# A fused kernel of retention attention, a soft mixture of experts and a bilinear block: PSUM handed out in tiles of two banks in the attention and in single banks behind it

## The chip, the cores and the metric

The kernel runs on one core of a Trainium2 chip, in one launch. The metric is the device time of that launch in microseconds (us); lower is better. The core has five engines that run side by side and wait for each other with semaphores: TensorE (PE in the profile; PEld is its weight load), VectorE (DVE), ScalarE (ACT), GpSimd (POOL) and SyncE (SP), which here only issues transfers. PE writes its products into PSUM, a memory of eight banks of 128 partitions x 512 float32 values; DVE and ACT read them from there.

## The reference

Three blocks, one behind the other, all in float32:

```python
# attention, 8 batches x 8 heads x 576 positions x 64
scores = (q @ k.T) / 8;  out = (scores * decay(i - j)) @ v        # causal, no softmax
x = out as (4608 tokens, 512 features)
# soft mixture of experts: 8 experts x 4 slots = 32 slots
logits = x @ phi
d = softmax over the tokens of logits
slot_in = d.T @ x;  slot_out[e] = relu(slot_in[e] @ w1[e]) @ w2[e]
x = softmax over the slots of logits @ slot_out
# bilinear block
y = (((x @ m1) * (x @ m2)) @ w3) @ w_out
```

## The kernel before

**Attention.** The 36 units are blocks of 128 tokens; 32 are main units, every ninth is a tail of half the work. In iteration u of the loop (`for u in range(NU)`) PE does, in this order: the product of unit u with the values (`emit_pv`, L280), the state update of unit u+1 (`emit_state`, L294), the scores of unit u+2 (`emit_qk`, L251), transposes (`emit_turns`, L213 and L217) and the part of unit u+1 that comes from the state (`emit_inter`, L314). DVE multiplies what PE left: `emit_xt` scales unit u's output (L328, into `xts`), `emit_p` puts the mask and decay on the scores of unit u+2 (L262, into `pm`). Both do it bank by bank, with two products each for a main unit: scores lie in banks 0 and 1, the output in banks 5 and 3 (of which 256 columns each). Order within an engine is the order of the code; nothing is rescheduled.

**Weights beside it.** The weights of the bilinear block come as 40 pieces in 64-bit floats and are converted beside the attention and the experts: ACT L489 and L491, DVE L490, L492, L484 (`conv_list`), POOL L510 (`add`), and for `wo` and `w3` also ACT L515 (`copy`) and POOL L520 (`sub`).

**Softmax over the tokens.** Every four units there are logits (`emit_logits`, L350, then three small DVE operations), exponentials on ACT, and a running sum `zacc` of one column (`emit_z`, L428) and running slots `acc` (`emit_slots`, `add_slots`, L445). Behind the loop the last logits, transposes (L340), slots and sums are finished: `zb` (L865, from `zacc` and `beta`), the product L866, L872 from `acc`, and `slotm`, from which the first expert starts (L587).

**Experts.** Per expert `emit_l1` (L587), `emit_l2` (L606), with weights that are loaded into every place that comes free (`load_expert`, L570), and products `w3 @ w_out` in between (`emit_Ws`, L551). A cast of w3 (ACT L515) waits until the L551 products on the place that it overwrites are done.

**Pairs.** Since the bilinear block acts on combinations of 32 slots, products of pairs of slots are built: L976 (`sot` with m1 into bank 7, then with m2 into bank 6), DVE transposes L982, and for each block `cb` of features DVE L1020, L1021, L1022 (`pairs`, in banks 7 and 2 in turn), ACT L1023, DVE L1027 (`pairs_low`), and 12 products on PE (`g_mm`, L1035). Behind block 0 stand 16 products into bank 6 (L1065). POOL prepares the first token tile meanwhile (`pair_prep`: L632, ACT L633, L635, then L628, ACT L629, L630).

**Last stage.** Nine token tiles T of four outputs each: for each T four products L1101, then per output 12 products L1110 to L1112, an eviction by ACT (L1114) and a store. The outputs go through the eight banks in the order below, so that a T with an even number begins with bank 7 and the T before it ends with bank 6.

**Banks.** Six banks are tiles of their own; banks 6 and 7 are the halves of one tile `pair`, which holds transposes in the attention:

```python
bank = [psum.tile([128, 512], F32, name=f"bank{i}") for i in range(6)]
pair = psum.tile([128, 1024], F32, name="pair")
bank += [pair[:, 0:512], pair[:, 512:1024]]
...
misc[:] = [bank[6], bank[7], bank[2], bank[4]]      # behind the attention: small products, in turn
...
return bank[(7, 2)[cb % 2]].rearrange("p (a b) -> p a b", b=32) if cb else ptmp[0][0]      # sums(cb)
...
obs = [bank[(7, 4, 2, 0, 1, 5, 3, 6)[(4 * T + tb) % 8]] for tb in range(4)]                # last stage
```

Of the kernel before, what the change touches and what calls it, by code (L numbers as in the profile page):

```python
# [9 lines left out]
F32 = mybir.dt.float32  # L10
# [6 lines left out]
ALU = mybir.AluOpType  # L17
# [14 lines left out]
def retention_softmoe_bilinear(  # L32
# [15 lines left out]
    nc = tc.nc  # L48
    const = ctx.enter_context(tc.tile_pool(name="const", bufs=1))
    tmp = ctx.enter_context(tc.tile_pool(name="tmp", bufs=1))  # L50
    psum = ctx.enter_context(tc.tile_pool(name="psum", bufs=1, space=bass.MemoryType.PSUM))
    dram = ctx.enter_context(tc.tile_pool(name="dram", bufs=1, space=bass.MemoryType.DRAM))

    expt = dram.tile([64 * NT, 512], F32, name="expt")
    bank = [psum.tile([128, 512], F32, name=f"bank{i}") for i in range(6)]
    pair = psum.tile([128, 1024], F32, name="pair")
    bank += [pair[:, 0:512], pair[:, 512:1024]]
    pools = {}

    def open_pool(name, side="left"):  # L60
        cm = tc.tile_pool(name=name, bufs=1, side=side, reuse_waits="tile")
        pools[name] = (cm, cm.__enter__())

    def close_pool(name):
        pools.pop(name)[0].__exit__(None, None, None)

    def new(pool, name, n, dt=F32, **kw):
        return pools[pool][1].tile([128, n], dt, name=name, **kw)

    cst = const.tile([128, 128 + 32 + 128], F32, name="cst")  # L70
    ident, isum = cst[:, 0:128], cst[:, 128:160]
# [64 lines left out]
    def tail(u):  # L136
        return items[units[u][0]][1] == 4
# [7 lines left out]
    def block_of(u):  # L145
        return items[units[u][0]][1]
# [76 lines left out]
    def qk_view(u, h):  # L223
        return bank[6 + h if u == 1 else h]
# [10 lines left out]
    def p_main(u):  # L235
        return p_places[u % 2].rearrange("p (h k t) -> p h k t", h=2, k=4)
# [17 lines left out]
    def emit_p(u):  # L254
        if tail(u):
            nc.vector.tensor_tensor(
                out=p_tail(u), in0=qk_view(u, 0).rearrange("p (x k i) -> p x k i", x=2, k=4),
                in1=ptail.unsqueeze(1).to_broadcast([128, 2, 4, 64]), op=ALU.mult,
            )
            return  # L260
        for h in range(2):
            nc.vector.tensor_tensor(  # L262
                out=p_main(u)[:, h], in0=qk_view(u, h).rearrange("p (k t) -> p k t", k=4), in1=mask_sb.unsqueeze(1).to_broadcast([128, 4, 128]), op=ALU.mult,
            )

    def emit_pv(u):
        x = units[u][1]
# [51 lines left out]
        return last  # L319

    def emit_xt(u):
        for r in range(2):
            ps = bank[(5, 3)[r]][:, 0:256].rearrange("p (k t) -> p k t", k=2)
            o, f = xts[u % 6][:, r::2], xtab_sb[block_of(u) % 4][:, r::2]
            if tail(u):
                o, ps = (t.rearrange("p k (x i) -> p k x i", x=2) for t in (o, ps))
                f = f[:, :, 0:64].unsqueeze(2).to_broadcast([128, 2, 2, 64])
            nc.vector.tensor_tensor(out=o, in0=ps, in1=f, op=ALU.mult)  # L328

    L = {"cc": []}  # L330
    misc = [bank[6], bank[7], bank[2]]
# [91 lines left out]
    def emit_z(T):  # L423
        _, al, zt = st[T]
        if T == 0:
            nc.vector.tensor_copy(zacc, zt)
        else:
            nc.vector.scalar_tensor_tensor(out=zacc, in0=zacc, scalar=al, in1=zt, op0=ALU.mult, op1=ALU.add)  # L428

    def emit_slots(T, add=True):  # L430
        dt = st["dt", T]
# [36 lines left out]
    def load_pieces():  # L468
        while nl[0] < len(pieces) and nl[0] < done[0] + NRAW:
            load_piece(nl[0])  # L470
            nl[0] += 1
# [167 lines left out]
    with tc.manual_schedule():  # L639
# [178 lines left out]
        free.extend([*kb, *p_places, s_place, kt_place])  # L818
        load_expert(4)
        load_pieces()  # L820
        misc[:] = [bank[6], bank[7], bank[2], bank[4]]
        nc.gpsimd.memset(slotm, 0.0)
        emit_logits(T)
# [272 lines left out]
        for T in range(NT):  # L1096
# [5 lines left out]
            for tb in range(4):  # L1102
# [12 lines left out]
                for o, i in stores(4 * T + tb):  # L1115
                    nc.sync.dma_start(out=o, in_=os[i])
        close_pool("place")


# [73 lines left out]
```

## Time and profile before

| | us |
|---|---|
| median of 3 runs | 412.31 (411.59 to 412.42) |
| the profiled execution's own time | 410.99 |
| its span in the trace | 409.3 |
| PE busy | 381.5 (93%) |
| DVE busy | 265.5 (65%) |
| ACT busy | 197.9 (48%) |
| POOL busy | 171.9 (42%) |

Shares of busy time are means over stages with different limits: the attention lasts to about 162 us, the experts to about 257, the pairs to about 295, the last stage to the end. The granted clock of PE is full in all 40 slices of the span. The mean share of the DMA engines is high until about 250 us and low behind that.

### The profile page before, as it was taken

To read this page: it belongs to the slowest core of one execution; us is meant where nothing else is said; L and a number is where in the kernel's file an instruction comes from. 1 tells how busy PE (TensorE), PEld (TensorE's weight loads), DVE (VectorE), ACT (ScalarE), POOL (GpSimd) and SP (SyncE) were. 2 spreads that over 40 slices of the span, in tenths; PEclk is the share of its full clock that TensorE was granted. 3 is DMA by queue.
4 is the path that set the end of the run, shared out by engine and by line. 5 is a ranking of instruction groups with operands and counts; after the bars stand their busy time and mean duration, and the time that the engine had idled before them with its cause. 6 is when DMAs were issued, how large, how long until landed. Compare 5 with 4: busy or idle time off the path is not lost.

```text
span 409.3 us, 11039 instructions
## 1 busy us (share of the span) xinstructions
PE 381.5 (93%) x4447; PEld 284.0 (69%) x4447; DVE 265.5 (65%) x504; ACT 197.9 (48%) x416; POOL 171.9 (42%) x158
## 2 busy tenths in 40 slices
PE   6999979999999998899999889989899999999996
PEld 4888867877988887565555444658587777777774
DVE  4659999999898996429757640469766434445500
ACT  2347777676767765235444412224444353544332
POOL 2635675655454463026335331126634333443320
PEclk9999999999999999999999999999999999999999
DMA  7999998799889887999999999680168979899434
GB/s 243 316 355 336 310 325 278 234 393 373 266 270 338 268 302 266 336 410 323 409 410 408 408 408 317 154 161 2 51 130 204 232 178 239 227 208 222 135 78 103
DMA packets 48211, 108.75 MB, mean 266 GB/s; under 512 B 7584, under 2 KB 10016, under 8 KB 48160
## 3 DMA queue, kind: packets, MB, share of 16 engines
q1 hardware_dynamic: 47008, 107.85, 82.1%
q8 instruction: 35, 0.57, 0.6%
q10 hardware_dynamic: 1152, 0.20, 0.3%
q14 instruction: 16, 0.13, 0.1%
HBM read 97.41 MB, written 10.62 MB: 264 GB/s over the span
## 4 chain that ended last, share of the span: by engine, by line
PE 60%; DVE 18%; DMA 15%; SPq 2%; issue 2%; ACT 2%; POOL 1%; ACTq 0%; POOLq 0%; DVEq 0%
PE bank L1110 6%; PE bank L1111 6%; PE bank L1112 6%; PE bank L551 5%; PE bank L251 5%; PE bank L280 5%; DMA kr<-in_v 4%; PE bank L314 3%; DVE pm L262 3%; DMA kt<-in_ew 3%; DMA k<-in_ew 2%; DMA expt<-et 2%; DVE vals L484 2%; PE pair L1110 2%; DMA xts<-in_ew 2%; PE bank L294 2%
## 5 line engine op out<-in xcount | busy, mean ns | idle before, releaser
L630 POOL TENSOR_TENSOR cc<-mw_sb,cc 128x512 fp32r<-128x512 f32 x36 | 46.0, 1296 | 58.6 <-ACT cc L629 58.6
L510 POOL TENSOR_TENSOR vals<-vals,msb 128x512 int32<-128x512 int32 x24 | 30.8, 1285 | 54.6 <-DVE vals L484 43.9
L551 PE MATMUL bank<-wop,w3p 128*128 128x512 f32 x192 | 50.5, 405 | 0.0
L262 DVE TENSOR_TENSOR pm<-bank,msb 128x512 f32<-128x512 f32 x62 | 39.8, 683 | 10.1 <-PE bank L251 9.8
L551 PEld LDWEIGHTS bank<-wop,w3p 128*128 128x128 f32 x192 | 34.4, 189 | 15.0 <-issue 8.7
L629 ACT CAST cc<-mw_sb 128x512 fp32r<-128x512 f32 x36 | 22.2, 616 | 43.5 <-DVE mw_sb L628 34.8
L251 PE MATMUL bank<-q,kt 64*128 64x128 f32 x496 | 36.4, 285 | 0.9 <-issue 0.9
L628 DVE TENSOR_TENSOR mw_sb<-lga,raw 128x512 f32<-128x512 f32 x32 | 29.3, 955 | 12.3 <-POOL cc L630 12.0
L280 PE MATMUL bank<-pm,v 128*64 128x128 f32 x512 | 35.4, 279 | 0.9 <-issue 0.6
L520 POOL TENSOR_TENSOR w3p<-vals,w3p 128x512 fp32r<-128x512 f32 x16 | 20.6, 1287 | 35.0 <-ACT w3p L515 33.1
L510 POOL TENSOR_TENSOR mw_sb<-mw_sb,msb 128x512 int32<-128x512 int32 x16 | 20.4, 1277 | 33.0 <-DVE mw_sb L484 23.4
L251 PEld LDWEIGHTS bank<-q,kt 64*128 64x128 f32 x496 | 30.3, 187 | 3.7 <-issue 1.6
L1110 PE MATMUL bank<-w3p,cc 128*128 128x512 f32 x81 | 32.0, 395 | 0.0
L280 PEld LDWEIGHTS bank<-pm,v 128*64 128x64 f32 x512 | 27.4, 136 | 6.2 <-issue 4.2
L1112 PE MATMUL bank<-w3p,cc 128*128 128x512 f32 x81 | 31.5, 389 | 0.0
L1111 PE MATMUL bank<-w3p,cc 128*128 128x512 f32 x81 | 31.5, 389 | 0.0
L218 ACT COPY kt<-pair 128x512 f32<-128x512 f32 x26 | 15.3, 589 | 27.4 <-PE pair L217 27.4
L491 ACT ACTIVATE msb<-raw 128x512 int32<-128x512 uint32 x40 | 28.0, 699 | 0.0
L190 POOL TENSOR_TENSOR k<-kr,msb 128x512 f32<-128x512 f32 (+1 forms) x30 | 25.6, 876 | 4.4 <-DMA kr<-in_v 2.6
L314 PE MATMUL bank<-q,st 64*64 64x128 f32 (+1 forms) x512 | 22.3, 269 | 4.7 <-DVE xts L328 4.2
L1035 PE MATMUL bank<-w,wop 128*128 128x512 f32 x96 | 23.4, 396 | 2.7 <-DVE wop L1027 2.7
L1114 ACT ACTIVATE mw_sb<-bank,rz 128x512 f32<-128x512 f32 x27 | 18.5, 686 | 12.7 <-PE bank L1112 6.4
(254 smaller groups left out, 818.5 us busy)
## 6 DMA issues: line engine op xcount, KB each, us to landing
q<-in_q SPq DMA_DIRECT2D x20, 512.0 KB, 6.3
raw<-expt SPq DMA_DIRECT2D x36, 256.0 KB, 4.3
kr<-in_v SPq DMA_DIRECT2D x16, 512.0 KB, 6.3
v<-in_v SPq DMA_DIRECT2D x16, 512.0 KB, 6.7
raw<-in_m SPq DMA_DIRECT2D x16, 512.0 KB, 6.3
raw<-in_w SPq DMA_DIRECT2D x16, 512.0 KB, 6.1
out_x<-mw_sb SPq DMA_DIRECT2D x64, 128.0 KB, 2.5
k<-in_ew SPq DMA_DIRECT2D x14, 512.0 KB, 10.1
```

Of the source, the lines that this page charges most:

```text
L251: last = nc.tensor.matmul(out=ps[:, p], lhsT=ktb[u % 2][a, p], rhs=Q[a, :, x, p], start=True, stop=True)
L262: nc.vector.tensor_tensor(out=p_main(u)[:, h], in0=qk_view(u, h).rearrange("p (k t) -> p k t", k=4), in1=mask_sb.unsqueeze(1).to_broadcast ...
L280: last = nc.tensor.matmul(out=xt_view(p)[side(p, h)], lhsT=v_tile(u)[:, 1 - h, x, p], rhs=p_main(u)[:, h, p], start=(block_of(u) == 0 and ...
L314: last = nc.tensor.matmul(out=xt_view(p)[side(p, h), 64 * y:64 * y + 64] if tail(u) else xt_view(p)[side(p, h)].rearrange("p (c i) -> p c ...
L491: lambda: nc.scalar.activation(out=p.bitcast(I32), in_=lo, func=ACTF.Copy, scale=2.0 ** -29),
L510: nc.gpsimd.tensor_tensor(out=ti, in0=ti, in1=parts[j % 2].bitcast(I32), op=ALU.add)
L551: nc.tensor.matmul(out=ps, lhsT=x, rhs=y, start=(k8 == 0 and part == 0), stop=(k8 == 7 and part == 2))
L628: eng.tensor_tensor(out=e, in0=x, in1=y[:, m], op=ALU.mult)
L630: nc.gpsimd.tensor_tensor(out=cl[m], in0=e, in1=ch[m], op=ALU.subtract)
L1110: nc.tensor.matmul(out=ob, lhsT=ch[m][:, sl], rhs=gh[m], start=False, stop=False)
L1111: nc.tensor.matmul(out=ob, lhsT=ch[m][:, sl], rhs=gl[m], start=False, stop=False)
L1112: nc.tensor.matmul(out=ob, lhsT=cl[m][:, sl], rhs=gh[m], start=False, stop=(m == 3))
```

## The change

PSUM becomes a pool that is opened twice. In the attention it holds three tiles of two banks (`scores`, `output`, `pair`) and two of one (`one`, `state`); the list `bank` maps the old numbers onto their halves. `emit_p` and `emit_xt` make one product of each pair of them, over both banks (tails stay as they were). Behind the attention the pool is closed and opened again with eight tiles of one bank. Apart from that `emit_z` moves from DVE to ACT.

```diff
--- before.py
+++ after.py
@@ -48,17 +48,13 @@
     nc = tc.nc
     const = ctx.enter_context(tc.tile_pool(name="const", bufs=1))
     tmp = ctx.enter_context(tc.tile_pool(name="tmp", bufs=1))
-    psum = ctx.enter_context(tc.tile_pool(name="psum", bufs=1, space=bass.MemoryType.PSUM))
     dram = ctx.enter_context(tc.tile_pool(name="dram", bufs=1, space=bass.MemoryType.DRAM))
 
     expt = dram.tile([64 * NT, 512], F32, name="expt")
-    bank = [psum.tile([128, 512], F32, name=f"bank{i}") for i in range(6)]
-    pair = psum.tile([128, 1024], F32, name="pair")
-    bank += [pair[:, 0:512], pair[:, 512:1024]]
     pools = {}
 
-    def open_pool(name, side="left"):
-        cm = tc.tile_pool(name=name, bufs=1, side=side, reuse_waits="tile")
+    def open_pool(name, side="left", **kw):
+        cm = tc.tile_pool(name=name, bufs=1, side=side, reuse_waits="tile", **kw)
         pools[name] = (cm, cm.__enter__())
 
     def close_pool(name):
@@ -66,6 +62,12 @@
 
     def new(pool, name, n, dt=F32, **kw):
         return pools[pool][1].tile([128, n], dt, name=name, **kw)
+
+    open_pool("psum", space=bass.MemoryType.PSUM)
+    scores, output, pair = (new("psum", n, 1024) for n in ("scores", "output", "pair"))
+    one, state = (new("psum", n, 512) for n in ("one", "state"))
+    b2 = lambda t: (t[:, 0:512], t[:, 512:1024])
+    bank = [*b2(scores), one, output[:, 512:1024], state, output[:, 0:512], *b2(pair)]
 
     cst = const.tile([128, 128 + 32 + 128], F32, name="cst")
     ident, isum = cst[:, 0:128], cst[:, 128:160]
@@ -258,10 +260,10 @@
                 in1=ptail.unsqueeze(1).to_broadcast([128, 2, 4, 64]), op=ALU.mult,
             )
             return
-        for h in range(2):
-            nc.vector.tensor_tensor(
-                out=p_main(u)[:, h], in0=qk_view(u, h).rearrange("p (k t) -> p k t", k=4), in1=mask_sb.unsqueeze(1).to_broadcast([128, 4, 128]), op=ALU.mult,
-            )
+        nc.vector.tensor_tensor(
+            out=p_places[u % 2].rearrange("p (g t) -> p g t", g=8), in0=(pair if u == 1 else scores).rearrange("p (g t) -> p g t", g=8),
+            in1=mask_sb.unsqueeze(1).to_broadcast([128, 8, 128]), op=ALU.mult,
+        )
 
     def emit_pv(u):
         x = units[u][1]
@@ -319,13 +321,17 @@
         return last
 
     def emit_xt(u):
+        o, f = xts[u % 6], xtab_sb[block_of(u) % 4]
+        if not tail(u):
+            by = lambda t: t.rearrange("p (k r) t -> p r k t", r=2)
+            nc.vector.tensor_tensor(out=by(o), in0=output.rearrange("p (r k t) -> p r k t", r=2, k=4)[:, :, 0:2], in1=by(f), op=ALU.mult)
+            return
         for r in range(2):
-            ps = bank[(5, 3)[r]][:, 0:256].rearrange("p (k t) -> p k t", k=2)
-            o, f = xts[u % 6][:, r::2], xtab_sb[block_of(u) % 4][:, r::2]
-            if tail(u):
-                o, ps = (t.rearrange("p k (x i) -> p k x i", x=2) for t in (o, ps))
-                f = f[:, :, 0:64].unsqueeze(2).to_broadcast([128, 2, 2, 64])
-            nc.vector.tensor_tensor(out=o, in0=ps, in1=f, op=ALU.mult)
+            ps = bank[(5, 3)[r]][:, 0:256].rearrange("p (k x i) -> p k x i", k=2, x=2)
+            nc.vector.tensor_tensor(
+                out=o[:, r::2].rearrange("p k (x i) -> p k x i", x=2), in0=ps,
+                in1=f[:, r::2, 0:64].unsqueeze(2).to_broadcast([128, 2, 2, 64]), op=ALU.mult,
+            )
 
     L = {"cc": []}
     misc = [bank[6], bank[7], bank[2]]
@@ -425,7 +431,7 @@
         if T == 0:
             nc.vector.tensor_copy(zacc, zt)
         else:
-            nc.vector.scalar_tensor_tensor(out=zacc, in0=zacc, scalar=al, in1=zt, op0=ALU.mult, op1=ALU.add)
+            nc.scalar.activation(out=zacc, in_=zacc, func=ACTF.Identity, scale=al, bias=zt)
 
     def emit_slots(T, add=True):
         dt = st["dt", T]
@@ -818,6 +824,9 @@
         free.extend([*kb, *p_places, s_place, kt_place])
         load_expert(4)
         load_pieces()
+        close_pool("psum")
+        open_pool("psum", space=bass.MemoryType.PSUM)
+        bank[:] = [new("psum", f"bank{i}", 512) for i in range(8)]
         misc[:] = [bank[6], bank[7], bank[2], bank[4]]
         nc.gpsimd.memset(slotm, 0.0)
         emit_logits(T)
@@ -1115,6 +1124,7 @@
                 for o, i in stores(4 * T + tb):
                     nc.sync.dma_start(out=o, in_=os[i])
         close_pool("place")
+        close_pool("psum")
 
 
 # ---- launch: one core; inputs laid out for the transfers, output as the reference has it ----
```

Three places, as the instructions stand in the built programs (a number behind a name tells buffers apart; what stands in brackets is waited for).

PE in the last stage, from one token tile to the next: `gs` and `cs` are the operands of L1101, `cc` those of L1110 (now L1119). Before:

```order
L1112 MATMUL pair_73<-g3_3491,cc13_3490 128x512
L1101 MATMUL pair_73<-gs_3492,cs_3482 128x512 [waits DVE_49,Activation_49]
L1101 MATMUL bank4_71<-gs_3492,cs_3482 128x512 [waits DVE_49]
L1101 MATMUL bank2_69<-gs_3492,cs_3482 128x512
L1101 MATMUL bank0_67<-gs_3492,cs_3482 128x512
L1110 MATMUL pair_73<-w3p_81,cc00_3483 128x512
```

and now:

```order
L1121 MATMUL bank6_2626<-g3_3437,cc13_3436 128x512
L1110 MATMUL bank7_2627<-gs_3438,cs_3428 128x512 [waits DVE_49]
L1110 MATMUL bank4_2624<-gs_3438,cs_3428 128x512 [waits DVE_49]
L1110 MATMUL bank2_2622<-gs_3438,cs_3428 128x512
L1110 MATMUL bank0_2620<-gs_3438,cs_3428 128x512
L1119 MATMUL bank7_2627<-w3p_79,cc00_3429 128x512 [waits Activation_49]
```

The wait for ACT at the first product is gone; the one at `cc` was implied by it before.

DVE in the stage of the pairs, blocks 1 and 2 (`bank4` and `msb` are the factors). Before:

```order
L1022 TENSOR_TENSOR bank2_69<-bank2_69,mw_sb_79 128x480 [waits DVE_49]
L1020 TENSOR_TENSOR mw_sb_79<-msb_86,bank4_71 128x480
L1021 TENSOR_TENSOR pair_73<-bank4_71,msb_86 128x512 [waits PE_49]
L1022 TENSOR_TENSOR pair_73<-pair_73,mw_sb_79 128x480 [waits DVE_49]
L1027 TENSOR_TENSOR wop_80<-bank2_69,wop_80 128x512 [waits Activation_49]
```

and now:

```order
L1031 TENSOR_TENSOR bank2_2622<-bank2_2622,mw_sb_77 128x480 [waits DVE_49]
L1029 TENSOR_TENSOR mw_sb_77<-msb_84,bank4_2624 128x480
L1030 TENSOR_TENSOR bank7_2627<-bank4_2624,msb_84 128x512
L1031 TENSOR_TENSOR bank7_2627<-bank7_2627,mw_sb_77 128x480 [waits DVE_49]
L1036 TENSOR_TENSOR wop_78<-bank2_2622,wop_78 128x512 [waits Activation_49]
```

The product into bank 7 (now L1030) no longer waits for PE.

ACT behind the attention, from `beta` to the first expert's `hr`. Before:

```order
L852 ACTIVATE beta_2757<-mn_2701,negm_2755 128x1 [waits DVE_49]
L515 CAST w3p_81<-vals_84 128x512 [waits PE_49]
L515 CAST w3p_81<-vals_84 128x512 [waits PE_49,Pool_49]
L592 ACTIVATE hr_2820<-bank0_67 128x256 [waits DVE_49,PE_49]
L559 CAST w0_2826<-bank5_72 128x512 [waits Activation_49]
```

and now:

```order
L861 ACTIVATE beta_2703<-mn_2647,negm_2701 128x1 [waits DVE_49]
L521 CAST w3p_79<-vals_82 128x512 [waits PE_49]
L521 CAST w3p_79<-vals_82 128x512 [waits PE_49,Pool_49]
L434 ACTIVATE zacc_76<-zacc_76,zt_2656,al_2659 128x1 [waits Activation_49]
L598 ACTIVATE hr_2766<-bank0_2620 128x256 [waits DVE_49,PE_49]
L565 CAST w0_2772<-bank5_2625 128x512 [waits Activation_49]
```

The sum `zacc` stands behind both casts of w3.

## Rows read from the trace of the kernel before

**Rows 1.** Chain of waits, in time: start us, us, piece.
```profile
70.31 0.67 DVE xts L328 x2
70.98 1.20 DVE pm L262 x2
...
216.24 11.03 DMA kt<-in_ew
```

**Rows 2.** Timeline, PE, last stage: start us, us, instruction [idle before, releaser].
```profile
307.19 0.39 PE L1112 MATMUL bank<-g,cc 128*128 128x512 f32 x1
307.51 0.73 PE L1101 MATMUL bank<-gs,cs 64*128 64x512 f32 x3
...
318.96 0.39 PE L1112 MATMUL pair<-g,cc 128*128 128x512 f32 x1
320.18 0.50 PE L1101 MATMUL pair<-gs,cs 64*128 64x512 f32 x1 [0.83 <-ACT mw_sb L1114]
```

**Rows 3.** Timeline, ACT, last stage.
```profile
319.44 0.69 ACT L1114 ACTIVATE mw_sb<-pair,rz 128x512 f32<-128x512 f32 x1 [1.65 <-issue]
```

**Rows 4.** Waits, 262 to 409 us: us in total, times, longest.
```profile
PE pair L1101 <- ACT mw_sb L1114: 3.3, 4, 0.8
```

**Rows 5.** Timeline, all engines, stage of the pairs.
```profile
260.97 1.93 PE L976 MATMUL pair<-mw_sb,sot 128*32 128x256 f32 x32 [0.64 <-DVE mw_sb L982]
...
269.75 3.84 PE L1065 MATMUL pair<-w,gs 128*64 128x512 f32 x16
...
273.63 0.70 DVE L1021 TENSOR_TENSOR pair<-bank,msb 128x512 f32<-128x512 f32 x1 [2.54 <-PE pair L1065]
...
275.67 15.59 PE L1035 MATMUL bank<-w,wop 128*128 128x512 f32 x66 [0.25 <-DVE wop L1027]
...
278.70 2.65 POOL L635 TENSOR_TENSOR cs<-mw_sb,cs 32x512 fp32r<-32x512 f32 x2 [8.90 <-ACT cs L633]
...
292.73 2.56 PE L1035 MATMUL bank<-w,wop 128*128 128x512 f32 x10 [1.47 <-DVE wop L1027]
```

**Rows 6.** Timeline, DVE, attention.
```profile
43.47 1.17 DVE L490 TENSOR_SCALAR vals<-vals 128x512 f32<-128x512 f32 x1
...
66.90 1.24 DVE L428 SCALAR_TENSOR_TENSOR zacc<-zacc,al,zt 128x1 f32<-128x1 f32 x1
...
77.51 0.42 DVE L490 TENSOR_SCALAR mw_sb<-mw_sb 128x512 f32<-128x512 f32 x1
...
152.65 0.90 DVE L428 SCALAR_TENSOR_TENSOR zacc<-zacc,al,zt 128x1 f32<-128x1 f32 x1
```

**Rows 7.** Timeline, POOL, attention.
```profile
43.06 1.30 POOL L520 TENSOR_TENSOR wop<-vals,wop 128x512 fp32r<-128x512 f32 x1
...
66.84 1.27 POOL L520 TENSOR_TENSOR wop<-vals,wop 128x512 fp32r<-128x512 f32 x1
```

**Rows 8.** Waits, 20 to 160 us.
```profile
PE bank L314 <- DVE xts L328: 3.4, 5, 1.3
```

**Rows 9.** Timeline, all engines, behind the attention.
```profile
164.52 1.06 PE L434 MATMUL pair<-xg,dt 128*32 128x512 f32 x8 [0.57 <-DVE mt L356]
...
166.19 0.30 ACT L377 ACTIVATE al<-mn,nm 128x1 f32<-128x1 f32 x1
...
170.27 0.33 PE L418 MATMUL pair<-cst,dd 128*128 128x128 f32 x1 [0.68 <-ACT xg L341]
...
172.41 0.28 DVE L865 TENSOR_SCALAR zb<-zacc,beta 128x128 f32<-128x128 f32 x1
...
172.86 3.70 PE L551 MATMUL bank<-wop,w3p 128*128 128x512 f32 x15
172.97 0.75 DVE L445 SCALAR_TENSOR_TENSOR acc<-acc,al,bank 128x512 f32<-128x512 f32 x1 [0.28 <-PE bank L434]
...
176.42 0.62 ACT L515 CAST w3p<-vals 128x512 fp32r<-128x512 f32 x1 [2.17 <-PE bank L551]
...
176.54 1.20 PE L872 MATMUL bank<-ib,acc 128*128 128x32 f32 x12
```

## The prediction

> **What bounds the kernel now.** I read the chain of waits first, then the waits by pair of engines, then the timelines of the stages in which the chain changes its engine. The chain runs through DVE in part of the attention (products L328 and L262 beside the conversions), through transfers in the second half of the experts (a load of 11.03 us at 216.24), and through PE in the last stage [rows 1, 2]. So the change has to be priced four times: in the attention, behind it, in the stage of the pairs, and in the last stage.
>
> The reader should look for one thing above all: waits that name the tile `pair` although the two instructions use different halves. In the last stage PE begins an even token tile with bank 7. At 307.51, in front of an odd one, it goes on 0.32 us after its last product began (307.19); at 320.18, in front of an even one, 1.22 us after (318.96) [rows 2]. In between ACT evicts bank 6, from 319.44 to 320.13, and PE starts 0.05 us behind that [rows 3]. Bank 7 itself was long free. The view of waits counts four of these, 3.3 us in all [rows 4]. In the stage of the pairs DVE L1021 writes bank 7 at 273.63, after 2.54 us of waiting, as soon as the 16 products L1065 are done (269.75 + 3.84 = 273.59); those write bank 6. And PE's second L976 (bank 6) waits 0.64 us for DVE's transposes of bank 7 [rows 5].
>
> **The change part by part.** *Eight banks of their own behind the attention.* The order of the changed program has lost these waits, and nothing else moved there.
>
> Last stage: each of four boundaries falls from 1.22 to 0.32 us: 4 x 0.90 = 3.6 us [rows 2, 4]. PE sets the end of this stage, so all of it counts. What would be late next is the operands `cc`, made for the next token tile by ACT and POOL. Were they late by the whole, nothing would be gained; but at the odd boundaries, where PE already goes on at once, they show no wait, so I take 3.6 whole, with 2.5 as the low end.
>
> Pairs: 0.64 us comes off ahead of everything in the stage. Then DVE gains 2.54 us. PE had its own work in that time (the 16 products), so it gains only what it later loses to a late DVE: 0.25 us at 275.67 and 1.47 us at 292.73 are shown as waits, 1.7 in all, and shorter ones may lie unseen inside the group of 66 products in 15.59 us [rows 5]. So the gain lies between 1.7 and 2.5, DVE's own; I take 2.2, since a row for the unseen part is missing and both ends are near. POOL is the other candidate for the end of this stage, but its work starts at 278.70 behind an 8.90 us wait for ACT's cast of `cs`, which stands behind a cast of the pairs that DVE made late [rows 5]. It moves with DVE. Together 2.8 us, between 0.6 and 3.2.
>
> *One product over two banks.* In the chain a pair of L262 takes 1.20 us from start to next start, a pair of L328 0.67 [rows 1]. So 512 columns cost 0.60 and 256 cost 0.335: 256 columns are 0.265, and the fixed part is 0.07 us. A merged unit saves 0.14 us, and 32 main units 4.5 us of DVE time. The Trainium skill (Perfetto Trace Analysis, Optimizing Scalar/DVE Operations) puts the access overhead of a DVE operation on PSUM at about 125 ns and advises to group operations where the engine is saturated. By that page the 64 merges would be worth 8.0 us of DVE time and the term below some 0.4 us more; the rows show about half of its overhead per operation, and I go by the rows.
>
> Little of it reaches the end. In most units of the first 80 us a conversion waits for POOL: L490 takes 0.42 us alone and 1.17 at 43.47, and ends 0.28 us behind the POOL product that began at 43.06 (44.64 against 44.36) [rows 6, 7]. POOL was started by the conversion before, not by the merged products, so DVE would come 0.14 us earlier and wait 0.14 us longer. I count 11 such units. From about 76 to 143 us the chain is PE's, and DVE's time is free there. So I take nothing for the merges themselves. They could give at most what PE waits for L328: 3.4 us in five waits [rows 8]. They could also cost: the state's products of the next unit may now begin only after the whole output is scaled, not after its first half. Where PE waits for it, the old second half ended 0.67 us after the start, the new whole after 0.60, so this is even; I put 0.3 us as the cost at worst.
>
> *`zacc` on ACT.* It took 1.24 us at 66.90 and 0.90 at 152.65 for one column, each ending with a POOL product (66.84 + 1.27 = 68.11 against 68.14) [rows 6, 7]. Without it the next conversion still meets POOL's end, but `acc` is done in the shadow. At 66.90 the conversion would have ended at 69.3 (68.14 + 0.75 + 0.42) and now ends at 68.11 + 0.28 = 68.4: 0.9 us, of which I take 0.7, in a stretch that DVE and POOL pace. At 152.65 I take 0.5. The other sums lie in PE's stretch. The attention: 1.2 us, between none and 3.4.
>
> *Behind the attention.* The last sum now stands on ACT behind the second cast of w3, which waits for PE's 15 products L551 until 176.42 [rows 9]. So: 176.42 + 0.62 = 177.04, the sum 0.30 (as long as `al`, also one column with a pointer operand) gives 177.34, `zb` 0.28 gives 177.62, and `acc` behind it on DVE 0.75 gives 178.37. PE wanted `acc` at 176.54 [rows 9]. That is 1.8 us lost, and the first expert waits for it. Against it two more waits on the halves of `pair` go: 0.57 us at 164.52 and 0.68 at 170.27 [rows 9], 1.25 us, ahead of the 15 products. New banks wait for the last use of the tiles whose place they take, which no row shows; I allow 0.05 us. Net +0.6 us, between -1.0 and +1.8. I pass this on to the end in full: the first expert frees places for loads, and the loads set the pace later (11.03 us in the chain [rows 1]).
>
> The sum against the profiled execution's own 410.99 us: -1.2 + 0.6 - 2.8 - 3.6 = -7.0, so 404.0. The median of the runs stands 1.3 us above that execution (412.31), so I predict 412.31 - 7.0 = 405.3 us.
>
> **The rivals.**
> *Only the last stage gains.* In the pairs another wait takes the place of the one removed: if ACT's cast of `cs` does not move, POOL still begins at 278.70, and PE, done with the pairs earlier, waits for `cs` and `cc` at the head of the last stage. For it: POOL waits for ACT there, 8.90 us [rows 5]. Against it: that cast stands on ACT behind casts which move with DVE. Only 0.6 of the 2.8 us remains: 412.31 - 4.8 = 407.5.
> *The merges pay in full.* If DVE, coming earlier, finds the gap between two POOL products and goes first, PE's waits of 3.4 us [rows 8] go and the sum behind the attention is hidden by the loads: -3.4 - 2.8 - 3.6 = -9.8, so 402.5. For it: gaps of POOL are common. Against it: 0.14 us is little beside the 0.41 us by which L490 comes after POOL's start (43.47 against 43.06) [rows 6, 7].
> *The banks stay tied.* If the separate banks still wait, through something that the order doesn't print, only attention and what follows remain: 412.31 - 1.2 + 1.8 = 412.9 at worst, 411.7 with the two waits behind the attention gone. Against it: the waits are missing in the program's own order.
> *Slower.* A product that crosses from one bank to the next could run slower than two that stay inside one; no row shows one. If it ran at half the rate, a merged L262 would take 2.2 us instead of 1.20 and L328 1.13 instead of 0.67, so 1.5 us more per unit on an engine that is full in the first 80 us: 32 units x 1.5 = 48, less about 10 of slack where PE paces, so about 443. It decides from about 0.22 us per unit, where 32 units cost the 7.0 won elsewhere. Against it: only that 256 and 512 columns scale as their columns do [rows 1].
>
> **How the numbers follow.** The forecast has 0.60, only the last stage 0.13, merges in full 0.15, banks tied 0.06, slower 0.06. The forecast's own range is 403.5 to 407: the terms' ends are partly opposed. Taking in the first two rivals and some of the spread behind the attention gives 402.3 to 408.3 for 8 times in 10. What a measurement of this kernel can tell from no change is about 0.2%, 0.8 us. Faster is the forecast and the first two rivals, 0.88; banks tied is the same, 0.06; slower 0.06.
>
> **What would show it.** Right: PE's step in front of even token tiles is 0.3 us in all four places; L1030 (the old L1021) into bank 7 starts without a wait while L1074 (the old L1065) runs, and no wait of over 1 us stands in front of the last products of the pairs; a merged scores product takes about 1.2 us, an output product about 0.7; the last `zacc` begins behind the second cast, and `zb` ends over 3 us later, counted from PE's slots product, than before. Wrong: an attention that ends over 3 us earlier or at all later than before; conversions that no longer end with POOL's products; a new wait for POOL in front of L1110 at the first token tile.

## The result, and the profile after

| | before | after |
|---|---|---|
| median, us | 412.37 (411.59 to 413.19, 4 runs) | 406.12 (404.52 to 407.16, 4 runs) |
| ratio | | 0.9845, 95% interval 0.9804 to 0.9886 |
| profiled execution, us | 410.99 | 406.82 |
| its span, us | 409.3 | 405.1 |

The forecast was 405.3 us within 402.3 to 408.3. The time is right, but one of its four terms, what is lost behind the attention, was put 1.8 us too low, and others made that good, which the medians alone don't show. So the span is cut into six stages at points that PE's timeline gives in every kernel. **A** ends with the first transposes behind the attention (L340, after: L346), **B** with the first expert's first product (L587, L593), **C** with its second layer (L606, L612), **D** with the products for the pairs (L976, L985), **E** with the last stage's first product (L1101, L1110), **F** with the last product started. us in each:

| kernel | A | B | C | D | E | F |
|---|---|---|---|---|---|---|
| before | 165.51 | 12.68 | 5.93 | 74.28 | 36.82 | 109.77 |
| after | 165.47 | 14.44 | 7.35 | 74.06 | 33.34 | 106.16 |
| difference | -0.04 | +1.76 | +1.42 | -0.22 | -3.48 | -3.61 |
| forecast | -1.8 | +1.2 (B and C) | | 0 | -2.8 | -3.6 |

The forecast's terms for the attention and for what lies behind it are -1.2 and +0.6. The first of the two false waits behind the attention (0.57 us at 164.52 [rows 9]) ends before A does, so its -0.6 stands in A here, and B and C keep +1.2.

The six differences add to -4.2 us, as the spans do. The medians lie 6.25 us apart: the profiled execution of before lies 1.4 us below the median of its kernel and that of after 0.7 above. Where executions of the same code begin to differ is taken up below, with the attention.

The last stage first. PE's timeline of after in front of token tile 2, an even one (start us, us, instruction):

```profile
318.41 0.39 PE L1121 MATMUL bank<-g,cc 128*128 128x512 f32 x1
318.73 0.73 PE L1110 MATMUL bank<-gs,cs 64*128 64x512 f32 x4
```

The step is 0.32 us where it was 1.22 [rows 2]. It is the same in front of all eight later tiles, and ACT's eviction of bank 6 (L1123, 318.88 to 319.57) now lies beside PE's work instead of in front of it.

The stage of the pairs, PE and DVE of after:

```profile
261.32 3.66 PE L985 MATMUL bank<-mw_sb,sot 128*32 128x256 f32 x64
...
271.81 3.83 PE L1074 MATMUL bank<-w,gs 128*64 128x512 f32 x16
275.49 19.24 PE L1044 MATMUL bank<-w,wop 128*128 128x512 f32 x84
294.66 1.25 PE L1110 MATMUL bank<-gs,cs 64*128 64x512 f32 x4
```
```profile
273.08 0.69 DVE L1030 TENSOR_TENSOR bank<-bank,msb 128x512 f32<-128x512 f32 x1
```

This answers [rows 5]: the 64 products with `sot` run in one piece, DVE's product into bank 7 begins while L1074 still writes bank 6, and the 84 products behind L1065, which came in groups of 8, 66 and 10 with waits of 0.25 and 1.47 us before the last two, follow in one group without a wait.

Behind the attention the first false wait is gone. PE of before, then of after, from the last logits (L350, L356) to the end of A:

```profile
162.86 1.08 PE L350 MATMUL pair<-xts,cst 128*32 128x128 f32 x32 [0.42 <-ACT xg L220]
165.51 1.09 PE L340 MATMUL bank<-cst,xts 128*128 128x128 f32 x8
```
```profile
163.60 1.08 PE L356 MATMUL bank<-xts,cst 128*32 128x128 f32 x32 [0.59 <-ACT dt L426]
165.47 1.09 PE L346 MATMUL bank<-cst,xts 128*128 128x128 f32 x8
```

That is 2.65 us and now 1.87, so 0.78 us came off, in A. What follows, PE, ACT, DVE and POOL of after, is to be held against [rows 9]:

```profile
171.90 3.72 PE L557 MATMUL bank<-wop,w3p 128*128 128x512 f32 x15
177.57 0.41 PE L875 MATMUL bank<-cst,zb 128*128 128x32 f32 x2 [1.96 <-DVE zb L874]
178.23 1.22 PE L881 MATMUL bank<-ib,acc 128*128 128x32 f32 x12 [0.25 <-DVE acc L451]
...
179.91 1.08 PE L593 MATMUL bank<-ew,slotm 128*32 128x256 f32 x8
180.76 1.93 PE L593 MATMUL bank<-kr,slotm 128*32 128x256 f32 x16
182.47 0.79 PE L593 MATMUL bank<-q,slotm 128*32 128x256 f32 x8
```
```profile
175.48 0.62 ACT L521 CAST w3p<-vals 128x512 fp32r<-128x512 f32 x1 [2.19 <-PE bank L557]
176.00 0.38 ACT L434 ACTIVATE zacc<-zacc,zt,al 128x1 f32<-128x1 f32 x1
```
```profile
176.42 1.10 DVE L874 TENSOR_SCALAR zb<-zacc,beta 128x128 f32<-128x128 f32 x1 [4.89 <-ACT zacc L434]
177.44 0.73 DVE L451 SCALAR_TENSOR_TENSOR acc<-acc,al,bank 128x512 f32<-128x512 f32 x1
```
```profile
176.18 1.26 POOL L526 TENSOR_TENSOR w3p<-vals,w3p 128x512 fp32r<-128x512 f32 x1 [1.48 <-ACT w3p L521]
```

The sum is late, as forecast. Two things are new. `zb` takes 1.10 us, not 0.28, and ends (177.52) with the POOL product beside it (177.44). And the first expert's products run at half pace behind the wait: 16 of them take 1.93 us in place of 1.05 in before. The granted clock says the same. The first row is before, the next three are after (window, its length, busy us of PE, PEld, DVE, ACT, POOL, the granted clock, DMA share, GB/s):

```profile
180.00:184.00 4.00, 3.77 (x19) 2.74 (x15) 1.90 (x6) 2.47 (x6) 0.00 (x0) 1.00 1.04 416
```
```profile
176.00:180.00 4.00, 2.13 (x19) 1.56 (x23) 2.50 (x5) 0.39 (x2) 1.26 (x1) 0.93 1.02 414
180.00:184.00 4.00, 4.00 (x36) 1.98 (x37) 0.00 (x0) 0.66 (x2) 0.00 (x0) 0.65 0.88 349
184.00:190.00 6.00, 5.64 (x34) 3.27 (x33) 4.62 (x12) 3.21 (x8) 1.60 (x2) 1.00 0.63 216
```

0.65 as a mean of 4 us means that TensorE stood at its lower level, 1.2 GHz, for most of them, after a stretch in which it had waited 2.2 us for `zb` and `acc`.

### The profile page after: what moved, and what is told of

Its sections match the earlier page's. It is cut to its first block, busy times and chain, and to the rows that moved or that the text cites. A ratio compares the mean times of both kernels' runs of the same rounds, so it can differ in the third digit from the quotient of the medians.

```text
span 405.1 us, 10964 instructions
## 1 busy us (share of the span) xinstructions
PE 382.5 (94%) x4447; PEld 286.0 (71%) x4447; DVE 260.7 (64%) x432; ACT 199.8 (49%) x424; POOL 172.1 (42%) x158
## 4 chain that ended last, share of the span: by engine, by line
PE 43%; DMA 7%; DVE 2%; ACT 1%; issue 0%; ACTq 0%; DVEq 0%; SPq 0%
PE bank L1119 9%; PE bank L1121 8%; PE bank L1120 8%; PE bank L557 5%; PE bank L1044 5%; DMA v<-in_ew 3%; DMA kt<-in_ew 3%; PE bank L612 2%; DMA k<-in_ew 2%; PE bank L593 2%; PE bank L1110 2%; PE bank L1074 1%; PE bank L985 1%; DVE w L566 0%; ACT w L565 0%
## 5 line engine op out<-in xcount | busy, mean ns | idle before, releaser
L557 PE MATMUL bank<-wop,w3p 128*128 128x512 f32 x192 | 52.0, 414 | 0.0
L263 DVE TENSOR_TENSOR pm<-scores,msb 128x1024 f32<-128x1024 f32 x31 | 37.8, 1219 | 12.8 <-PE scores L253 12.5
L1119 PE MATMUL bank<-w3p,cc 128*128 128x512 f32 x108 | 43.1, 399 | 0.0
L1121 PE MATMUL bank<-w3p,cc 128*128 128x512 f32 x108 | 42.1, 390 | 0.0
L1120 PE MATMUL bank<-w3p,cc 128*128 128x512 f32 x108 | 42.0, 389 | 0.0
L253 PE MATMUL scores<-q,kt 64*128 64x128 f32 x496 | 37.3, 290 | 0.0
L282 PE MATMUL output<-pm,v 128*64 128x128 f32 x512 | 35.2, 279 | 1.1 <-issue 1.0
L1123 ACT ACTIVATE mw_sb<-bank,rz 128x512 f32<-128x512 f32 x36 | 24.7, 685 | 20.1 <-PE bank L1121 11.3
L253 PEld LDWEIGHTS scores<-q,kt 64*128 64x128 f32 x496 | 31.1, 192 | 3.0 <-issue 1.1
L282 PEld LDWEIGHTS output<-pm,v 128*64 128x64 f32 x512 | 27.4, 136 | 6.3 <-issue 4.5
L316 PE MATMUL output<-q,st 64*64 64x128 f32 (+1 forms) x512 | 20.1, 268 | 6.5 <-DVE xts L327 4.5
L1119 PEld LDWEIGHTS bank<-w3p,cc 128*128 128x128 f32 x108 | 20.3, 188 | 7.1 <-issue 2.9
```

Of the source, the lines that this page charges most:

```text
L253: last = nc.tensor.matmul(out=ps[:, p], lhsT=ktb[u % 2][a, p], rhs=Q[a, :, x, p], start=True, stop=True)
L263: nc.vector.tensor_tensor(out=p_places[u % 2].rearrange("p (g t) -> p g t", g=8), in0=(pair if u == 1 else scores).rearrange("p (g t) -> p ...
L282: last = nc.tensor.matmul(out=xt_view(p)[side(p, h)], lhsT=v_tile(u)[:, 1 - h, x, p], rhs=p_main(u)[:, h, p], start=(block_of(u) == 0 and ...
L557: nc.tensor.matmul(out=ps, lhsT=x, rhs=y, start=(k8 == 0 and part == 0), stop=(k8 == 7 and part == 2))
L1119: nc.tensor.matmul(out=ob, lhsT=ch[m][:, sl], rhs=gh[m], start=False, stop=False)
L1120: nc.tensor.matmul(out=ob, lhsT=ch[m][:, sl], rhs=gl[m], start=False, stop=False)
```

## The experiments

All ratios are against the kernel before, run on the same chip beside them. The stages of all kernels, as in the table above:

| kernel | median, us | ratio (95%) | A | B | C | D | E | F |
|---|---|---|---|---|---|---|---|---|
| e1 banks alone | 403.88 | 0.981 (0.978 to 0.984) | 165.06 | 11.78 | 5.93 | 74.54 | 33.37 | 106.19 |
| e2 merges alone | 411.25 | 0.9977 (0.9956 to 0.9997) | 165.95 | 12.68 | 5.93 | 74.23 | 36.83 | 109.76 |
| e3 `zacc` alone | 413.90 | 1.0051 (1.0025 to 1.0076) | 166.58 | 15.84 | 7.79 | 73.39 | 36.80 | 109.76 |
| e4 all but `zacc` | 402.99 | 0.979 (0.976 to 0.983) | 165.13 | 11.78 | 5.94 | 74.09 | 33.34 | 106.19 |
| e5 last sum early | 402.77 | 0.978 (0.975 to 0.982) | 165.92 | 11.78 | 5.93 | 74.33 | 33.35 | 106.19 |
| e6 PE kept busy | 403.99 | 0.983 (0.979 to 0.986) | 163.78 | 14.44 | 5.93 | 73.91 | 33.34 | 106.16 |
| e7 order of banks | 409.40 | 0.9933 (0.9909 to 0.9957) | 166.53 | 12.66 | 5.93 | 73.76 | 36.80 | 106.95 |
| e8 four products | 412.04 | 1.0000 (0.9982 to 1.0018) | 166.71 | 12.70 | 5.92 | 73.80 | 36.80 | 109.76 |
| e9 warm start | 401.47 | 0.9746 (0.9722 to 0.9769) | 163.54 | 11.79 | 5.92 | 74.74 | 33.36 | 106.16 |
| e10 e5, no merges | 402.05 | 0.9764 (0.9738 to 0.9789) | 165.41 | 11.79 | 5.93 | 73.89 | 33.31 | 106.19 |
| e11 e5 again | 401.87 | 0.9753 (0.9727 to 0.9778) | 164.25 | 11.79 | 5.93 | 75.04 | 33.35 | 106.19 |

B, C, E and F come out alike within 0.1 us wherever the code is alike, but for C behind a late sum and F in e7; A and D do not. That is what makes the parts separable.

**The banks alone.** The kernel before, its tiles and products as they are, with the pool closed and opened again behind the attention:

```diff
+        close_pool("psum")
+        open_pool("psum", space=bass.MemoryType.PSUM)
+        bank[:] = [new("psum", f"bank{i}", 512) for i in range(8)]
         misc[:] = [bank[6], bank[7], bank[2], bank[4]]
```

> The kernel before with one part of the change alone: the pool of banks is closed behind the attention and opened again with eight banks of their own. Two-bank products and the sum on ACT are left out; bank 6 and 7 stay halves of one tile in the attention. Theory A (the gain is the false waits between halves of `pair`): 1.25 us behind the attention, 3.5 in the pairs and 3.6 in the last stage, 412.4 - 8.4 = 404.0 us, so faster than the whole change, since the late sum is missing. Rival B (the two-bank products pay, the loads hide what happens behind the attention): only pairs and last stage, 412.4 - 7.1 = 405.3, and the two-bank products bring the rest elsewhere.

403.88 us: the banks alone have a lower median than the whole change. B gives 0.90 us, E 3.45, F 3.58, in all 7.9 of the 8.2 by which the medians differ. To these come 0.78 us in A, where PE goes from the last logits to L341 in 1.87 us (163.19 to 165.06), as in after; so behind the attention 1.68 us came, more than the 1.25 read from the two waits.

**The merges alone.** The changed kernel, with two edits taken back:

```diff
-        bank[:] = [new("psum", f"bank{i}", 512) for i in range(8)]
+        six = [new("psum", f"bank{i}", 512) for i in range(6)]
+        two = new("psum", "two", 1024)
+        bank[:] = [*six, two[:, 0:512], two[:, 512:1024]]
...
-            nc.scalar.activation(out=zacc, in_=zacc, func=ACTF.Identity, scale=al, bias=zt)
+            nc.vector.scalar_tensor_tensor(out=zacc, in0=zacc, scalar=al, in1=zt, op0=ALU.mult, op1=ALU.add)
```

> The changed kernel with the two-bank products alone: behind the attention the reopened pool holds six banks and one tile of two (banks 6 and 7 as halves again), and the running sum is back on VectorE. Theory A: DVE's 0.14 us per unit ends in longer waits for POOL, the false waits are back: 412.4 us, within 0.8. Rival B (the merges give 3 us, as the changed kernel's logits moved from 3 us late at unit 8 to level at the end of the attention): 409.4.

411.25 us, 0.03 to 0.44% below before: within 1 us of nothing, and the false waits of E and F are back to the hundredth. The two-bank products themselves cost what the forecast said. The groups of products on DVE between 20 and 143 us (busy us, mean ns, then idle time before them), in after:

```profile
L263 DVE TENSOR_TENSOR pm<-scores,msb 128x1024 f32<-128x1024 f32 x26 | 31.7, 1219 | 6.2 <-PE scores L253 5.9
...
L327 DVE TENSOR_TENSOR xts<-output,slotm 128x512 f32<-128x512 f32 x13 | 8.9, 684 | 2.4 <-PE output L282 2.4
```

From start to next start a unit's scores take 1.13 us here (66.72 to 67.85 below) and took 1.20 [rows 1], so 0.07 us per merge. Where it can pay is seen at one place, the running sum of [rows 6] at 66.90. DVE and POOL of this kernel:

```profile
66.72 1.22 DVE L263 TENSOR_TENSOR pm<-scores,msb 128x1024 f32<-128x1024 f32 x1
67.85 0.21 DVE L434 SCALAR_TENSOR_TENSOR zacc<-zacc,al,zt 128x1 f32<-128x1 f32 x1
```
```profile
66.68 1.28 POOL L516 TENSOR_TENSOR vals<-vals,msb 128x512 int32<-128x512 int32 x1 [1.96 <-DVE vals L490]
67.92 1.29 POOL L526 TENSOR_TENSOR wop<-vals,wop 128x512 fp32r<-128x512 f32 x1
```

DVE comes 0.07 us before POOL's second product, and the sum takes 0.21 us in place of 1.24. The next conversion then waits instead (L496 takes 0.86 us where L490 took 0.41 in before), so this unit ends 0.7 us earlier against its start. That is the mechanism of the rival "the merges pay in full", at one unit of 32, and it is about what the median gained.

**`zacc` alone.** The kernel before with the one line of the running sum on ACT.

> The kernel before with the running sum `zacc` on ACT and nothing else. Theory A: the last sum stands behind the second cast of w3, which waits for the 15 products on PE; the wait costs 1.8 us and TensorE's clock falls in it, which costs the first expert's products another 1.4 us (in the changed kernel the five first groups took 3.3 us in place of 1.9); in the attention 1.2 us come back at most: 412.4 + 3.2 - 0.6 = 415.0 us. Rival C (the loads set the pace behind it and hide the loss): 412.4 or a little less.

413.90 us, 0.25 to 0.76% slower than before: this part of the change alone is a loss, of 2.1 us by the ratio where 2.6 were expected. B is 3.16 us longer and C 1.86; of these D gives 0.89 back. The granted clock of this kernel, behind the wait:

```profile
182.00:186.00 4.00, 3.96 (x34) 1.48 (x34) 0.29 (x1) 0.00 (x0) 0.00 (x0) 0.50 0.37 146
```

**All but `zacc`.** The changed kernel with the sum back on DVE.

> The changed kernel with the running sum `zacc` back on VectorE; two-bank products and separate banks stay. Theory A: the late sum goes and the clock stays up, 406.1 - 3.2 + 0.6 = 403.5 us, 0.5 within the run with the banks alone. Rival B (merges pay 3 us): 401. Rival C (loads hide the loss behind the attention): 406.1 to 406.7.

402.99 us: B and C are those of the banks alone, which are 2.66 and 1.41 us shorter than those of after. The median lies 3.1 us below that of after; what differs is within the spread of A. The loads do not hide the late sum.

**The place in ACT's queue.** The changed kernel with the call moved, nothing else:

```diff
         emit_slots(T, False)
+        emit_z(T)
         free.extend(xt_places)
...
         run_conv(5)
-        emit_z(T)
```

> The changed kernel with the last sum `zacc` issued on ACT ahead of the two casts of w3, right behind the last slots' products; all sums stay on ACT. Theory A (its place in ACT's queue costs the time, not ACT): `zb` no longer waits, l1 follows the attention's last transposes in 11.8 us as with the sum on VectorE (14.4 in the changed kernel), the first expert runs at the full clock: 403.0 us. Rival (ACT itself, or its port, makes the sum late): 405 to 406.

402.77 us. ACT of this kernel does the sum before the casts, `zb` takes 0.28 us (at 172.02, before any product of POOL), and PE no longer waits for it:

```profile
171.62 0.37 ACT L434 ACTIVATE zacc<-zacc,zt,al 128x1 f32<-128x1 f32 x1
173.11 0.62 ACT L521 CAST w3p<-vals 128x512 fp32r<-128x512 f32 x1 [1.13 <-PE bank L557]
```
```profile
175.91 0.30 PE L875 MATMUL bank<-cst,zb 128*128 128x32 f32 x2
```

So it was the place behind the second cast, not ACT.

**The clock.** The changed kernel with two unused products in PE's wait:

```diff
+        for _ in range(2):
+            nc.tensor.matmul(out=bank[7], lhsT=ident, rhs=xgs[0], start=True, stop=True)
         nc.tensor.matmul(out=bank[1][:, 0:32], lhsT=zb, rhs=isum, start=True, stop=True)
```

> The changed kernel with two unrelated 128x512 products on TensorE (into bank 7, not read) in the 2 us in which it waits for `zb`. Theory A (the wait costs twice: its own 1.8 us, and 1.4 us of half clock in the first expert behind it): the wait stays, the clock stays up, the first expert's products take 1.9 us instead of 3.3, so 406.1 - 1.4 = 404.7 us. Rival (the products of the first expert were slow for another reason, a port or the loads): no gain, 406.1 or up to 0.5 more.

403.99 us. B is as long as in after, 14.44, so the wait is the same; C falls from 7.35 to 5.93. PE and the granted clock:

```profile
178.22 0.64 PE L593 MATMUL bank<-ew,slotm 128*32 128x256 f32 x8 [0.19 <-DVE slotm L888]
178.68 1.05 PE L593 MATMUL bank<-kr,slotm 128*32 128x256 f32 x16
```
```profile
180.00:184.00 4.00, 3.80 (x19) 2.73 (x15) 1.87 (x5) 2.44 (x6) 0.00 (x0) 1.00 0.97 373
```

1.42 us is thus the price of the clock alone, as stage C shows. The medians can't show it: they lie 2.1 us apart, and the intervals of the two ratios overlap (0.979 to 0.986, after 0.9804 to 0.9886).

**The last stage without new banks.** The kernel before with two banks exchanged in the order of the outputs:

```diff
-            obs = [bank[(7, 4, 2, 0, 1, 5, 3, 6)[(4 * T + tb) % 8]] for tb in range(4)]
+            obs = [bank[(7, 4, 6, 0, 1, 5, 3, 2)[(4 * T + tb) % 8]] for tb in range(4)]
```

> The kernel before with banks 6 and 2 exchanged in the order of the last stage's outputs (7, 4, 6, 0, 1, 5, 3, 2), so that bank 7 no longer follows bank 6; they stay halves of one tile. Theory A: the four waits of 0.9 us go and nothing else changes: 412.1 - 3.6 = 408.5 us, with the pairs stage as long as before (36.8 us). Rival (in the last stage the separate banks gained in another way, or the operands `cc` are late next): 411 to 412.

409.40 us: F gives 2.82 us with no pool reopened, E nothing. The step in front of tile 2 is the short one:

```profile
319.99 0.39 PE L1112 MATMUL bank<-g,cc 128*128 128x512 f32 x1
320.31 0.49 PE L1101 MATMUL pair<-gs,cs 64*128 64x512 f32 x1
```

The 0.8 us that are missing to 3.6 lie mostly in the first tile (12.85 us from its first product to the next tile's, 12.29 in after). There the view of waits has another one between the halves, since banks 7 and 6 now serve the same tile (us in total, times, longest):

```profile
PE pair L1110 <- ACT mw_sb L1114: 0.3, 1, 0.3
```

**The opposite of the merges.** The kernel before with each product of the scores cut in two, 64 more of them than before and 96 more than after:

```diff
         for h in range(2):
-            nc.vector.tensor_tensor(
-                out=p_main(u)[:, h], in0=qk_view(u, h).rearrange("p (k t) -> p k t", k=4), in1=mask_sb.unsqueeze(1).to_broadcast([128, 4, 128]), op=ALU.mult,
-            )
+            for s in (slice(0, 2), slice(2, 4)):
+                nc.vector.tensor_tensor(
+                    out=p_main(u)[:, h, s], in0=qk_view(u, h).rearrange("p (k t) -> p k t", k=4)[:, s], in1=mask_sb.unsqueeze(1).to_broadcast([128, 2, 128]), op=ALU.mult,
+                )
```

> The kernel before with the scores' products of VectorE in four of 256 columns instead of two of 512, the opposite of the change: two more fixed parts of 0.07 us in each of 32 units, 4.5 us of VectorE time. Theory A (conversions wait for POOL and take up such differences, as the merged products gave only 1.1 us of 4.5): 1 to 2 us later, 413 to 414. Rival (VectorE's time counts in full in the attention): 416.5. Rival (nothing of it counts): 412.1.

412.04 us, ratio 1.0000: nothing of 4.5 us of DVE time reaches the end, within 0.7 us. My 1 to 2 us were wrong on this; waits take up even more than I thought. The same sum, DVE and POOL:

```profile
67.55 1.41 DVE L263 TENSOR_TENSOR pm<-bank,msb 128x256 f32<-128x256 f32 x4
68.88 1.09 DVE L429 SCALAR_TENSOR_TENSOR zacc<-zacc,al,zt 128x1 f32<-128x1 f32 x1
```
```profile
68.68 1.27 POOL L521 TENSOR_TENSOR wop<-vals,wop 128x512 fp32r<-128x512 f32 x1
```

The scores take 0.13 us more than [rows 1] has, the sum 0.15 less than in [rows 6], and it ends with POOL (69.97 against 69.95) as it did before.

**A warm start.** From e5, with one product on PE in its wait between the first transposes:

```diff
         load_k(2)
+        warm(256)
         emit_kt(1)
```

> The changed kernel with the last sum early on ACT, and one more unused product of 256 columns on TensorE between the first two groups of transposes, where it waits 0.7 us for ACT. In two of the executions looked at so far, the one of the changed kernel and one of a kernel with the attention as before, the first scores' 16 products took 2.08 us instead of 1.16 and the attention began about 1.5 us late. Theory A (TensorE's pace at the start is a matter of the single execution and of what it did before): the scores take 1.16 us in this one, time 402.8 or up to 0.7 less, with a smaller spread. Rival: the slow start comes from the two-bank tiles, 2.08 us again and no change.

The first scores in five kernels: before, after, e7 and e10 (whose attention is that of before but for the sums), e9:

```profile
8.76 1.16 PE L251 MATMUL bank<-q,kt 64*128 64x128 f32 x16
```
```profile
9.77 2.08 PE L253 MATMUL scores<-q,kt 64*128 64x128 f32 x16
```
```profile
9.51 2.08 PE L251 MATMUL bank<-q,kt 64*128 64x128 f32 x16
```
```profile
9.52 2.08 PE L252 MATMUL bank<-q,kt 64*128 64x128 f32 x16
```
```profile
8.89 1.16 PE L253 MATMUL scores<-q,kt 64*128 64x128 f32 x16
```

The slow start is found with and without two-bank tiles (after and e4, e7 and e10), and with two-bank tiles and no extra product the quick one is found too (e2, e5, e6 and e11, 1.16 us). So the change does not cause it, and the 1.16 us of e9 do not show that the extra product prevents it. With the slow start the profiled execution of after came to its first product with the values 2.10 us later than that of before (13.65 against 11.55). The granted clock of 7 to 14 us stands as 1.00 in all of them, so here only the products' durations tell. e9 has the lowest median of all, 401.47 us, but can't be told from e11 (0.9746 against 0.9753, the intervals overlap), so that the extra product helps the total is not shown either.

**The merges once more.** e1 with all sums on ACT and the last one early, so that against e5 only the products differ.

> The kernel before with the separate banks behind the attention and all sums on ACT, the last of them early; the two-bank products are left out. Against the next kernel only the products differ. Theory A (VectorE's 4.5 us are taken up by waits, since four times as many products cost nothing either): 402.8 to 403.5, within 0.8 of the next. Rival B (the products give 1 us, as the run with them alone had it): 403.8.

And e5 beside it on the same chip:

> The changed kernel with the last sum early on ACT, once more, beside the two others on the same chip: 402.8 us.

402.05 and 401.87 us: with the banks separate and the sum early, the two-bank products make no difference that can be measured.

## Why the prediction was right, and where it was not

**The false waits.** The mechanism was right in all places. The last stage was to give 3.6 us and gave 3.61; `cc` was not late next. The pairs were to give 2.8, at most 3.2, and gave 3.48: from L976 to the 16 products L1065 0.86 us came off where 0.64 were read, and behind them 2.62, so all of DVE's 2.54 us, where I took 2.2 because PE had its own work in that time. Behind the attention 1.25 us were read from two waits, and 0.78 came in A and 0.90 in B. The rival "only the last stage" is refuted by E, "the banks stay tied" by e1, "slower" by the 1219 ns of a product over two banks, and "the merges pay in full" by e2.

**The late sum.** This is the step that failed: "Net +0.6 us, between -1.0 and +1.8". B and C together became 3.18 us longer; less the 0.78 that came off ahead of them the net was +2.4, outside its own bounds. The place of the wait was right, its size was not. The wait itself cost 2.66 us (14.44 against 11.78 in B), not 1.8. Of the difference 0.82 us is `zb`, which takes 1.10 us at its new time, beside a product of POOL (in after and in e3), and 0.28 where no such product runs (in before, at 172.41, and in e5); that the product is the cause is read from this, no run moves it alone. And I did not ask what PE's clock does when PE waits, so a whole term is missing: 1.42 us in C, shown by e6. The Trainium skill (SBUF — State Buffer, Who interferes with whom) says that a DVE instruction with two SBUF inputs contends with a POOL instruction that reads SBUF, and that who issues first decides; the running sum agrees with it, 0.21 us just ahead of a POOL product and 1.24 behind one. By that rule the last sum could have stayed on DVE, where no POOL product runs before the casts, and e4 bears that out, with 0.21 us for it.

**The attention.** 1.2 us were to come off, 0.7 of them at the sum at 66.90 and 0.5 at the one at 152.65. Stage A hides whether they did: it spreads by 2.1 us between four executions of like attention (after, e5, e6, e11: 163.78 to 165.92), and that spread is there by 39 us, when DVE scales the output of unit 6 (37.14 to 39.22). Part of it comes from a load: a conversion of ACT waits for a piece of `wo` until 35.9 us in after and e5 and until 34.6 and 34.75 in e11 and e6. ACT of e5, then of e6:

```profile
35.93 0.68 ACT L495 ACTIVATE vals<-raw 128x512 f32<-128x512 f32 x1 [3.27 <-DMA raw<-in_wo]
```
```profile
34.75 0.70 ACT L495 ACTIVATE vals<-raw 128x512 f32<-128x512 f32 x1 [2.46 <-DMA raw<-in_wo]
```

Behind that the stretches with the two sums can be told apart. DVE scales the outputs of units 6 and 14, in before and in after:

```profile
36.47 0.75 DVE L328 TENSOR_TENSOR xts<-bank,xtab 128x256 f32<-128x256 f32 x2
75.65 0.75 DVE L328 TENSOR_TENSOR xts<-bank,xtab 128x256 f32<-128x256 f32 x2
```
```profile
39.22 0.68 DVE L327 TENSOR_TENSOR xts<-output,xtab 128x512 f32<-128x512 f32 x1
77.44 0.68 DVE L327 TENSOR_TENSOR xts<-output,xtab 128x512 f32<-128x512 f32 x1
```

The same in all kernels, and for units 30 and 34 (us from start to start):

| stretch | before, e1, e7, e8 | sum on ACT: e3, e10 | merges: e2, e4 | both: after, e5, e6, e9, e11 |
|---|---|---|---|---|
| unit 6 to 14 | 39.15 to 39.18 | 38.43 and 38.44 | 38.23 and 38.27 | 38.22 to 38.26 |
| unit 30 to 34 | 17.31 to 17.32 | 16.69 | 17.26 and 17.27 | 16.64 to 17.45 |

So the sum on ACT alone gives 0.7 and 0.6 us, close to the forecast, by the mechanism that was forecast. The merges alone give 0.9 in the first stretch, for which I took nothing, but do not add to it: with either change the sum no longer costs its 1.24 us behind POOL (in e2 and e4 it takes 0.21, at 67.85 and 68.22). At the second sum they do not bring DVE ahead of POOL, it takes 1.04 us in both (at 153.04 and 152.84), and there they give nothing. Between units 14 and 30 all kernels take 66.0 to 67.2 us, without an order. That most of DVE's 4.5 us is taken up by waits is shown by e8 and by e10 against e11. In stage A of after these gains, and the 0.78 us of the false wait, are hidden by a beginning that was 2.75 us later than that of before (39.22 against 36.47). One sign that I gave for "wrong", an attention that ends "at all later than before", came true for that reason: the last transposes of the loop began at 162.29 instead of 161.72.

**Passing on to the end.** I passed the delay behind the attention on in full. From the earliest to the latest begin of the second layer (e9 at 181.25, e3 at 190.21) stage D shrinks by 1.35 us, so about 85% passes through, an estimate from these two executions. Rival C of the experiments, that the loads hide the delay, is refuted by e4.

**The total.** By medians the change gives 6.25 us of the 7.0 forecast, by the profiled pair 4.2, and 6.9 if the 2.75 us of the later beginning are left out. The part behind the attention was 1.8 us too cheap; of that 0.7 is made good by the pairs, 0.2 by D, and the rest by the attention behind unit 6, which gave 2.0 us where 1.2 were forecast, 0.4 of them in stretches where no gain can be told from the spread. That these errors cancel is luck. What is shown is that the change with its sum left on DVE, or done early on ACT, is faster than the change: by 4.1 us in B and C. By the ratios to the kernel before it is 2.1 us in e4, 2.5 in e5 and 3.8 in e11, where only the interval of e11 lies clear of that of after.

## What to carry to other kernels

Look in the timelines for waits whose two instructions touch different halves of one tile: each is worth its whole length where its engine sets the end, and giving the halves tiles of their own, or just exchanging two banks in an order, removes it. When an operation moves to another engine, read what stands ahead of it in that queue and what runs beside it at its new time, and if TensorE has to wait for it, add the clock behind the wait. Time saved on an engine that meets another at every step is only worth something where it changes who comes first.

## What the runs showed of the hardware

- A wait of 2.2 us of PE in two pieces (1.96 and 0.25) was followed by half pace for some 4 us: granted clock 0.65 there, 1.00 with two unused products in the wait; price 1.42 us.
- At the start of a program PE's pace differs from one execution to the next: 16 products in 2.08 us in after and 1.16 in e5, e6 and e11, with the same code ahead of them, and a granted clock of 1.00 in the profile of each.
- A product of DVE that crosses from one bank of PSUM to the next runs at the rate of one that does not: 1024 columns over two banks take 1.13 us from start to next start, two products of 512 take 1.20, so the merge saves 0.07 us.
- A one-column operation of DVE took 0.21 us, or 1.24 where a POOL product had begun just before it, with whose end it ended; a `zb` of 128 columns took 0.28 us alone and 1.10 beside a POOL product.
